# Where layer one's last sums are split, and when layer two's first pair takes its second products

## The chip, the cores and the metric

The kernel runs on one core of one Trainium2 chip. The metric is the device time of one execution in microseconds; less is better. The median of three runs of the kernel before is 566.02 us (565.81 to 566.04).

## What is computed

A retention (a linear attention with a decaying state, 8 heads, 768 steps, batch 2) gives `x`, 1536 tokens of 512 numbers. Two feed-forward layers follow, each 512 to 2048 to 512, in float32:

```python
def _moe_ref(x, w_in, w_out):
    h = x @ w_in
    g = np.maximum(h, 0.0) + np.log1p(np.exp(-np.abs(h)))
    return (g @ w_out).astype(np.float32)
...
def _moe2_ref(x, w_in, w_out, s, b):
    h = x @ w_in
    r = np.maximum(h, 0.0)
    g = s * (r * r) + b
    return (g @ w_out).astype(np.float32)
...
    x = _moe_ref(x=x, **moe_kwargs)
    return _moe2_ref(x=x, **moe2_kwargs)
```

## The kernel before

**Parts.** Every factor of a large product is split into a high part (a rounded copy, `xh`, `wh`, `gh`) and a low part (the rest, `xl`, `wl`, `gl`), and a product is the sum of three: high by high, high by low, low by high. The rounded copy is made on ScalarE and the subtraction mostly on GpSimd (`split`, L110); a weight of 128 x 512 is first put together from two 32-bit words by `split_w` (L277) in four steps: a shift on VectorE (L290); a merge of words on VectorE (L292) with a scaled copy on ScalarE (L295, "the word half") and the load of another raw weight on the SP queue; a second merge on VectorE (L300); and the split.

**Tiles and pairs.** The 1536 tokens are three tiles of 512 (0, 1, 2). The 2048 hidden numbers are taken 128 at a time, and in layer two in pairs of these (p = 0 to 7). For a pair and a tile there are *first products* (the hidden numbers, into one bank of PSUM), the curve (in layer two a relu L559, a square L584, a scaled identity L585, then the split into `gh` and `gl`), and *second products*, which add to four banks of PSUM, the accumulators; there is one set of accumulators. After a pair's two halves, four instructions *take* the accumulators to `xa` of the tile on VectorE (L621 for the first pair, a copy, and L623 later, an addition). A full block of either kind is twelve matmuls of 512 columns.

**The layer change.** Layer one ends with the last steps of tile 2, whose second products run while layer two's first pair has begun. Its sum (accumulators plus what stands in `xa[2]`) is tile 2's input of layer two. The first pair of layer two is done by `plain` (L953, called in L1165), the later pairs by `second` (L981), which saves products by sums of tiles and weights: it starts with half blocks of six matmuls, copies their banks to SBUF on ScalarE (L508, `p1`, `p5`, `u2`) and joins them on VectorE (L552).

`plain` goes through six blocks k = 0 to 5, the halves 0 and 1 of tiles 0, 1 and 2. In this text F0 to F5 are their first products, and Sjh the second products of tile j, half h, of this first pair. A block's first products go to a bank of PSUM from the list `banks` (`h`, `y`, or `third`, written as None), and the relu frees that bank. Per block, in the program's order: the first products (L502), the relu (`begin`), the rest of the curve and the split of `gh` and `gl` (`finish`), the last step of the previous weight split (`end_part`), second products from the list `accs`, three steps of the next weight split (`go(work, 3)`), and sums and parts of tiles (`sums`, `parts`). In block 2 the last second products of layer one (`end`, L1157) come right after F2: two banks, their sums to `xa[2]` on VectorE (`sum_last`, L423), two more banks, their sums, and then `parts_last`: four copies to `xh[2]` on ScalarE (L428) and four subtractions to `xl[2]` on VectorE (L430). F4 and F5 read these.

The order around the change is thus: F0, two blocks of layer one's second products with F1 and F2 between them, `end`, F3, S00, F4, S01 with its four take copies, F5, and then `second` for the next pair (L981): a half block into `h`, copied as `p1`; a half block into `third` (L998), joined with `p1`; S10 (L1003); a half block into `y`, copied as `p5`; one into `h`, copied as `u2`; S11 with its take; two more half blocks; and so on. In the meantime the sum of tiles x4 is made on VectorE in block 3 (L448; its high part `x4h` on ScalarE, L485, and its low parts `x4l` on GpSimd, L488), and two sums of quarters of tile 2 in block 4 (L538).

Each engine works through its own queue in the order of the program (`manual_schedule`); engines wait for each other only where data or a bank, or a buffer, requires it.

Of the kernel before, what the change touches and what calls it, by code (L numbers as in the profile page):

```python
# [7 lines left out]
F32 = mybir.dt.float32  # L8
F32R = mybir.dt.float32r
U32 = mybir.dt.uint32  # L10
AF = mybir.ActivationFunctionType
ALU = mybir.AluOpType
# [10 lines left out]
NTILE = NT // TT  # L23
CPT = TT // C
KC = DM // P
# [23 lines left out]
def tile_retention_mlps(ctx: ExitStack, tc: tile.TileContext, head, w1, w2, sb, out):  # L49
    nc = tc.nc  # L50
# [18 lines left out]
    def bank(pool, tag):  # L69
        return pool.tile([P, 512], F32, tag=tag, name=tag)  # L70
# [19 lines left out]
    xh = [cp.tile([P, KC, TT], F32R, tag=f"xh{j}", name=f"xh{j}") for j in range(NTILE)]  # L90
    xl = [cp.tile([P, KC, TT], F32R, tag=f"xl{j}", name=f"xl{j}") for j in range(NTILE)]
    xa = [cp.tile([P, KC, TT], F32, tag=f"xa{j}", name=f"xa{j}") for j in range(NTILE)]
# [240 lines left out]
    steps = [(0, g, j, f4) for g in range(NG) for j in range(NTILE) for f4 in range(FG)]  # L333
# [7 lines left out]
    h_t, l_t, gg_t, acc_t = {}, {}, {}, {}  # L341
# [76 lines left out]
    def sum_last(banks):  # L418

        la, g, j, _ = steps[NS - 1]  # L420
        for cc in banks:
            t = xa[j][:, cc]
            nc.vector.tensor_tensor(out=t, in0=acc_t[la, g, j][cc], in1=t, op=ALU.add)  # L423

    def parts_last():
        j = NTILE - 1
        for cc in range(KC):
            nc.scalar.activation(xh[j][:, cc], xa[j][:, cc], AF.Copy)  # L428
        for cc in range(KC):
            nc.vector.tensor_tensor(  # L430
                out=xl[j][:, cc], in0=xa[j][:, cc], in1=xh[j][:, cc].bitcast(F32), op=ALU.subtract
            )

    x_t, x3 = {}, {}

# [42 lines left out]
    def parts_x(k, la=1):  # L478
        hi, lo = both(k)
        if k == 3 or k == 4 and not la:  # L480
            src = [x3[c] for c in range(2)]
            for c in range(2):
                nc.scalar.activation(hi[:, c], src[c], AF.Copy)
        else:
            nc.scalar.activation(hi, x_t[k], AF.Copy)  # L485
            src = [x_t[k][:, c] for c in range(2)]
        for c in range(2):
            nc.gpsimd.tensor_tensor(out=lo[:, c], in0=src[c], in1=hi[:, c].bitcast(F32), op=ALU.subtract)  # L488
        x_t[k] = hi, lo
# [9 lines left out]
    def all_of(ps, w, j):  # L499
        ops = [(a, b, k) for k in range(KC) for a, b in ((0, 0), (0, 1))] + [(1, 0, k) for k in range(KC)]  # L500
        for i, (a, b, k) in enumerate(ops):
            nc.tensor.matmul(  # L502
                ps, w[a][:, k * P : (k + 1) * P], (xh, xl)[b][j][:, k], start=i == 0, stop=i == len(ops) - 1
            )
# [41 lines left out]
    def next_t():  # L546
        turn[0] ^= 1
        return tp.tile([P, TT], F32, tag="t2" if turn[0] else "t1", name="c")
# [6 lines left out]
    def begin(la, src, own=False, by_pool=True, tags=None):  # L555

        if la:
            c = src if own else next_t()
            nc.scalar.activation(c, src, AF.Relu)  # L559
            return src, c, None  # L560
        if tags:
            r, u = (late.tile([P, TT], F32, tag=tag, name=tag) for tag in tags)
        else:
            r, u = next_t(), None
        if by_pool:
            nc.scalar.activation(r, src, AF.Relu)
            return src, r, u if tags else src if own else next_t()
        nc.vector.tensor_scalar(
            out=r.bitcast(U32), in0=src.bitcast(U32), scalar1=0x80000000, scalar2=None, op0=ALU.bitwise_or
        )  # L570
        nc.scalar.activation(r, r, AF.Softplus)
        return src, r, None
# [8 lines left out]
    def finish(la, p, half, j, of):  # L581
        src, c, u = of
        if la:
            nc.scalar.activation(c, c, AF.Square)  # L584
            nc.scalar.activation(c, c, AF.Identity, scale=sbt[:, 0:1], bias=sbt[:, 1:2])  # L585
        elif u is not None:
            nc.gpsimd.tensor_tensor(out=c, in0=c, in1=u, op=ALU.add)  # L587
            late_parts.append((la, p, half, j, c))
            return
        else:  # L590
            nc.vector.scalar_tensor_tensor(out=c, in0=src, scalar=0.0, in1=c, op0=ALU.max, op1=ALU.add)
        parts_g(la, p, half, j, c)
# [3 lines left out]
    def parts_g(la, p, half, j, c):  # L596
        gg_t[la, p, half, j] = gh, gl = next_g()
        split(gh, gl, c, nc.scalar, nc.gpsimd)

    def acc_2(la, p, j, half, banks=FIRST + SECOND):  # L600
        wh, wl = w_t[la * NF + 2 * p + half, 1]
        gh, gl = gg_t[la, p, half, j]
        if (la, p, "pair", j) not in acc_t:
            acc_t[la, p, "pair", j] = sums()[0]
        for some in ((0, 1), (2,)):
            for cc in banks:
                cs = slice(cc * P, (cc + 1) * P)
                if la:
                    ops = ((gh[:, cs], wh), (gl[:, cs], wh), (gh[:, cs], wl))
                else:  # L610
                    ops = ((wh[:, cs], gh), (wh[:, cs], gl), (wl[:, cs], gh))
                for i in some:
                    nc.tensor.matmul(  # L613
                        acc_t[la, p, "pair", j][cc], *ops[i], start=half == 0 and i == 0, stop=half == 1 and i == 2
                    )

    def take_2(la, p, j, banks=range(KC)):
        for cc in banks:
            ps, dst = acc_t[la, p, "pair", j][cc], xa[j][:, cc, :]
            if la and p == 0:  # L620
                nc.vector.tensor_copy(dst, ps)  # L621
            else:
                nc.vector.tensor_tensor(out=dst, in0=ps, in1=dst, op=ALU.add)  # L623
            if la and p == PAIRS - 1:
                r0 = j * TT + cc * P
                nc.sync.dma_start(out=out[r0 : r0 + P, :], in_=dst)

    NS = len(steps)
# [54 lines left out]
    def go(work, n):  # L683
        for _ in range(n):
            next(work, None)
# [54 lines left out]
    work, left = [iter(())], [0]  # L740
# [13 lines left out]
    with tc.manual_schedule():  # L754
# [130 lines left out]
        work = iter(())  # L885
# [6 lines left out]
        def part(to):  # L892

            nonlocal late_work, work
            late_work, work = work, split_next(to)
# [8 lines left out]
        def end_part():  # L904
            while late_parts:
                parts_g(*late_parts.pop(0))
            go(late_work, 1)
# [34 lines left out]
        def of_pair(la, p, j, half):  # L942
            def take(banks):
                if half:
                    take_2(la, p, j, banks)

            return lambda banks: acc_2(la, p, j, half, banks), take

        def whole(acc, take):
            acc(FIRST + SECOND)  # L950
            take(FIRST + SECOND)

        def plain(la, p, left, sums, parts):  # L953

            w = la * NF + 2 * p
            base = at[la, p + 1]
            accs = left + [lambda: whole(*of_pair(la, p, 0, 0)), lambda: whole(*of_pair(la, p, 0, 1)), lambda: None]
            banks = [(ps_h, "h"), (ps_y, "y"), None, (ps_h, "h"), None, (ps_y, "y")]
            for k, (j, half) in enumerate((j, half) for j in range(NTILE) for half in range(2)):
                part(base + k + 2 if la or k > 1 else 0)  # L960
                to = bank(*banks[k]) if banks[k] else bank_2[1]
                all_of(to, w_t[w + half, 0], j)
                if la and k == 2:
                    end_part()
                    accs[k]()
                of = begin(la, to, by_pool=False)
                if not la:
                    end_part()
                    go(work, 2)
                finish(la, p, half, j, of)  # L970
                if la:
                    end_part()
                if not la or k != 2:
                    accs[k]()
                go(work, 3 if la else 1)
                for x in sums[k]:
                    next(x, None)
                for x in parts[k]:
                    parts_x(x, la)
# [147 lines left out]
        for s in range(SB, GS):  # L1127
            accs = [of_step(s - LAG)]
# [7 lines left out]
        left = [lambda s=s: whole(*of_step(s)) for s in range(GS - LAG, GS)]  # L1136
# [5 lines left out]
        for s in range(S1, NS):  # L1142
            k = s - S1
            if k < 4:
                accs = [of_pair(0, P1 - 1, 1 + k // 2, k % 2)]
            else:
                accs = [of_step(s - LAG)] if k > 4 else [of_step(S1), of_step(S1 + 1)]
# [15 lines left out]
        left = [lambda s=s: acc_mm(s, FIRST + SECOND) for s in range(NS - LAG, NS - 1)] + [end]  # L1163
# [4 lines left out]
        p = PAIRS - 1  # L1168
# [6 lines left out]
        cc, r0 = KC - 1, NT - P  # L1175
# [90 lines left out]
```

## Time and profile before

| | |
|---|---|
| median of three runs | 566.02 us |
| the profiled execution, its own time | 565.88 us |
| its span in the profile | 564.0 us |
| TensorE busy | 557.2 us, 99% of the span |
| VectorE, ScalarE, GpSimd busy | 68%, 62%, 62% |
| mean granted clock of TensorE | 0.999 |
| chain that ended last | TensorE 92%, GpSimd 4%, ScalarE 2%, VectorE 1% |

The span is the time from the first to the last instruction that the profiler saw; the execution's own time is 1.9 us longer. Times in the rows below count from the start of the span. A timeline row gives the start, the duration, the engine (PE is TensorE, DVE VectorE, ACT ScalarE, POOL GpSimd), the line, the operation, what it writes and reads, and in brackets how long the engine stood still before it and what released it. Neighbouring instructions of one kind are one row ("x4"). Matmuls overlap, so a row's duration is longer than its distance to the next.

### The profile page before, as it was taken

The numbers are of one execution on the slowest core, as the hardware profiler recorded it, in microseconds if no ns is written. First come the engines' busy times: TensorE is split into PE (matmuls) and PEld (weight loads), VectorE is DVE, ScalarE is ACT, GpSimd is POOL, SyncE is SP. The second block draws the span as 40 slices with busy tenths as digits, with TensorE's granted clock in tenths as the row PEclk, the third lists the DMA queues.
The fourth block names the chain that finished last, engine by engine and source line by source line (L and its number), as shares of the span: only waits on it lengthen the run. The fifth ranks groups of instructions, "written<-read, shape, count | busy, mean of one in ns | idle before, by whom it ended". The sixth has DMA issues, their size and how long they took to land.

```text
span 564.0 us, 8397 instructions
## 1 busy us (share of the span) xinstructions
PE 557.2 (99%) x3098; PEld 465.4 (83%) x3098; DVE 383.7 (68%) x581; ACT 349.4 (62%) x641; POOL 348.9 (62%) x293
## 2 busy tenths in 40 slices
PE   8999999999999999999999999999999999999997
PEld 7877888888888888888888777888888888888886
DVE  4887768776757759786859887675665665656334
ACT  3766673544554665543437878858687776868561
POOL 4457467776598797733525999647566555646230
PEclk9999999999999999999999999999999999999999
DMA  8986112101222213322212022222211221110005
GB/s 342 405 355 223 41 38 65 48 29 48 74 76 73 76 37 111 115 76 77 73 38 76 0 74 76 76 74 76 75 63 53 74 74 41 73 38 2 0 11 213
DMA packets 15016, 50.61 MB, mean 90 GB/s; under 512 B 1792, under 2 KB 2048, under 8 KB 14976
## 3 DMA queue, kind: packets, MB, share of 16 engines
q1 hardware_dynamic: 14976, 50.08, 25.1%
q8 instruction: 24, 0.39, 0.3%
q14 instruction: 16, 0.13, 0.1%
HBM read 46.93 MB, written 3.15 MB: 89 GB/s over the span
## 4 chain that ended last, share of the span: by engine, by line
PE 92%; POOL 4%; ACT 2%; DVE 1%; issue 1%; DVEq 0%
PE acc L613 33%; PE acc L403 11%; PE h L494 9%; PE y L494 8%; PE h L352 8%; PE third L494 5%; PE y L352 4%; PE y L502 3%; PE third L502 2%; PE y L191 2%; PE s L172 2%; PE h L502 1%; PE h L191 1%; POOL gl L115 1%; PE acc L775 1%
## 5 line engine op out<-in xcount | busy, mean ns | idle before, releaser
L115 POOL TENSOR_TENSOR wl<-wm,wh 128x512 fp32r<-128x512 f32 x64 | 84.6, 1322 | 101.0 <-ACT wh L112 101.0
L115 POOL TENSOR_TENSOR gl<-c,gh 128x512 fp32r<-128x512 f32 x69 | 91.0, 1324 | 70.3 <-ACT gh L112 48.5
L623 DVE TENSOR_TENSOR xa<-acc,xa 128x512 f32<-128x512 f32 x131 | 82.3, 683 | 71.4 <-PE acc L613 71.2
L613 PE MATMUL acc<-wh,gl 128*128 128x512 f32 x190 | 74.3, 391 | 0.0
L613 PE MATMUL acc<-wh,gh 128*128 128x512 f32 x190 | 74.1, 390 | 0.0
L613 PE MATMUL acc<-wl,gh 128*128 128x512 f32 x190 | 53.9, 390 | 0.0
L112 ACT ACTIVATE gh<-c 128x512 fp32r<-128x512 f32 x69 | 43.6, 632 | 10.9 <-POOL c L587 6.9
L295 ACT ACTIVATE wm<-raw 128x512 f32<-128x512 f32 x64 | 42.4, 663 | 8.7 <-POOL wl L115 8.6
L300 DVE SCALAR_TENSOR_TENSOR wm<-wm,cu,word 128x512 uint32<-128x512 uint32 x54 | 39.9, 739 | 4.1 <-ACT wm L295 3.4
L292 DVE SCALAR_TENSOR_TENSOR word<-raw,cu,word 128x512 uint32<-128x512 uint32 x54 | 40.8, 756 | 1.9
L613 PEld LDWEIGHTS acc<-wl,gh 128*128 128x128 f32 x190 | 35.7, 188 | 7.6
L112 ACT ACTIVATE wh<-wm 128x512 fp32r<-128x512 f32 x64 | 39.7, 620 | 3.2 <-DVE wm L300 3.0
L613 PEld LDWEIGHTS acc<-wh,gl 128*128 128x128 f32 x190 | 35.8, 188 | 6.6
L613 PEld LDWEIGHTS acc<-wh,gh 128*128 128x128 f32 x190 | 35.8, 188 | 6.4
L585 ACT ACTIVATE c<-c,sbt 128x512 f32<-128x512 f32 x48 | 39.2, 816 | 1.6
L365 ACT ACTIVATE t<-t 128x512 f32<-128x512 f32 x24 | 15.1, 629 | 38.9 <-DVE t L359 38.9
L403 PE MATMUL acc<-gh,wh 128*128 128x512 f32 x96 | 37.9, 395 | 0.0
L403 PE MATMUL acc<-gl,wh 128*128 128x512 f32 x96 | 37.4, 390 | 0.0
L613 PE MATMUL acc<-gh,wh 128*128 128x512 f32 x96 | 37.3, 389 | 0.0
L613 PE MATMUL acc<-gl,wh 128*128 128x512 f32 x96 | 37.3, 389 | 0.0
L290 DVE TENSOR_SCALAR word<-raw 128x512 uint32<-128x512 uint32 x54 | 37.0, 686 | 0.4
L559 ACT ACTIVATE c<-c 128x512 f32<-128x512 f32 x21 | 13.1, 633 | 33.6 <-DVE c L552 33.6
(265 smaller groups left out, 1461.4 us busy)
## 6 DMA issues: line engine op xcount, KB each, us to landing
raw<-w SPq DMA_DIRECT2D x64, 512.0 KB, 3.5
qk<-head SPq DMA_DIRECT2D x12, 512.0 KB, 8.3
kv<-head SPq DMA_DIRECT2D x12, 512.0 KB, 8.4
out<-xa SPq DMA_DIRECT2D x11, 256.0 KB, 2.1
cst<-head SPq DMA_DIRECT2D x1, 518.0 KB, 4.4
cst<-head SPq DMA_DIRECT2D x1, 256.0 KB, 5.4
out<-xa SPq DMA_DIRECT2D x2, 128.0 KB, 1.8
sbt<-sb SPq DMA_DIRECT2D x1, 1.0 KB, 10.3
```

The source lines that it names most:

```text
L112: nc.scalar.activation(hi, src, AF.Copy)
L115: lo_eng.tensor_tensor(out=lo, in0=src, in1=hi.bitcast(F32), op=ALU.subtract)
L290: nc.vector.tensor_scalar(out=x, in0=lw, scalar1=29, scalar2=None, op0=ALU.logical_shift_right)
L292: nc.vector.scalar_tensor_tensor(out=x, in0=hw, scalar=cu[:, 0:1], in1=x, op0=ALU.bitwise_and, op1=ALU.bitwise_or)
L295: nc.scalar.activation(m, hw.bitcast(F32), AF.Copy, scale=REBIAS)
L300: nc.vector.scalar_tensor_tensor(out=m.bitcast(U32), in0=m.bitcast(U32), scalar=cu[:, 1:2], in1=x, op0=ALU.logical_shift_left, op1=ALU.bit ...
L352: nc.tensor.matmul(ps, w[:, cc * P : (cc + 1) * P], r[j][:, cc, :], start=i == 0, stop=i == len(ops) - 1)
L403: nc.tensor.matmul(acc_t[la, g, j][cc], *ops[i], start=f4 == 0 and i == 0, stop=ends(s) and i == 2)
L494: nc.tensor.matmul(ps, w[a][:, k * P : (k + 1) * P], x[b][:, k], start=start and i == 0, stop=i == len(ops) - 1, skip_group_check=True,)
L585: nc.scalar.activation(c, c, AF.Identity, scale=sbt[:, 0:1], bias=sbt[:, 1:2])
L613: nc.tensor.matmul(acc_t[la, p, "pair", j][cc], *ops[i], start=half == 0 and i == 0, stop=half == 1 and i == 2)
L623: nc.vector.tensor_tensor(out=dst, in0=ps, in1=dst, op=ALU.add)
```

## The change

Five things, all for layer two's first pair. `sum_last` leaves the sums in the accumulators' banks instead of `xa[2]`. `parts_last` makes the high and low parts from the banks. A new function `whole_last` copies the sums from the banks to `xa[2]` on ScalarE, after block 2's relu. The list of second products is moved one block later: none in block 3, S00 in block 4, S01 and its take in block 5; and to go with it the banks of F4 and F5 are exchanged (F4 to `y`, F5 to `third`). The three split steps of a block come ahead of its second products instead of behind them.

```diff
         la, g, j, _ = steps[NS - 1]
         for cc in banks:
-            t = xa[j][:, cc]
-            nc.vector.tensor_tensor(out=t, in0=acc_t[la, g, j][cc], in1=t, op=ALU.add)
+            t = acc_t[la, g, j][cc]
+            nc.vector.tensor_tensor(out=t, in0=t, in1=xa[j][:, cc], op=ALU.add)
 
     def parts_last():
-        j = NTILE - 1
+        la, g, j, _ = steps[NS - 1]
+        ps = acc_t[la, g, j]
         for cc in range(KC):
-            nc.scalar.activation(xh[j][:, cc], xa[j][:, cc], AF.Copy)
+            nc.scalar.activation(xh[j][:, cc], ps[cc], AF.Copy)
         for cc in range(KC):
-            nc.vector.tensor_tensor(
-                out=xl[j][:, cc], in0=xa[j][:, cc], in1=xh[j][:, cc].bitcast(F32), op=ALU.subtract
-            )
+            nc.vector.tensor_tensor(out=xl[j][:, cc], in0=ps[cc], in1=xh[j][:, cc].bitcast(F32), op=ALU.subtract)
+
+    def whole_last():
+        la, g, j, _ = steps[NS - 1]
+        for cc in range(KC):
+            nc.scalar.activation(xa[j][:, cc], acc_t[la, g, j][cc], AF.Copy)
...
-            accs = left + [lambda: whole(*of_pair(la, p, 0, 0)), lambda: whole(*of_pair(la, p, 0, 1)), lambda: None]
+            own_accs = [lambda: whole(*of_pair(la, p, 0, 0)), lambda: whole(*of_pair(la, p, 0, 1))]
+            accs = left + ([lambda: None] + own_accs if la else own_accs + [lambda: None])
             banks = [(ps_h, "h"), (ps_y, "y"), None, (ps_h, "h"), None, (ps_y, "y")]
+            if la:
+                banks[4:] = banks[:3:-1]
             for k, (j, half) in enumerate((j, half) for j in range(NTILE) for half in range(2)):
...
                 of = begin(la, to, by_pool=False)
+                if la and k == 2:
+                    whole_last()
                 if not la:
                     end_part()
                     go(work, 2)
                 finish(la, p, half, j, of)
                 if la:
                     end_part()
+                    go(work, 3)
                 if not la or k != 2:
                     accs[k]()
-                go(work, 3 if la else 1)
+                if not la:
+                    go(work, 1)
                 for x in sums[k]:
                     next(x, None)
                 for x in parts[k]:
                     parts_x(x, la)
```

## Rows read from the trace of the kernel before

**Rows 1.** The page, part 1: busy us (share of the span) and instructions.

```profile
PE 557.2 (99%) x3098; PEld 465.4 (83%) x3098; DVE 383.7 (68%) x581; ACT 349.4 (62%) x641; POOL 348.9 (62%) x293
```

**Rows 2.** Waits of TensorE, whole span: us in total, times, longest.

```profile
PE h L494 <- ACT p L508: 1.1, 1, 1.1
```

**Rows 3.** Timeline of TensorE: start us, us, engine, line, operation [idle before <-releaser].

```profile
316.58 0.39 PE L502 MATMUL h<-xh,wh 128*128 128x512 f32 x1
...
319.30 0.39 PE L613 MATMUL acc<-wh,gh 128*128 128x512 f32 x1
...
324.18 0.50 PE L502 MATMUL third<-xl,wh 128*128 128x512 f32 x1 [0.41 <-DVE xl L430]
...
336.33 0.39 PE L494 MATMUL y<-x1h,sh 128*128 128x512 f32 x1
...
338.96 0.50 PE L494 MATMUL h<-x2h,sh 128*128 128x512 f32 x1 [1.11 <-ACT p L508]
...
343.91 0.50 PE L494 MATMUL y<-xh,sh 128*128 128x512 f32 x1 [0.57 <-ACT p L508]
...
346.76 0.39 PE L613 MATMUL acc<-wh,gh 128*128 128x512 f32 x1
```

**Rows 4.** Timeline of ScalarE, 318 to 344 us.

```profile
318.48 0.58 ACT L559 ACTIVATE c<-third 128x512 f32<-128x512 f32 x1
...
324.84 0.66 ACT L295 ACTIVATE wm<-raw 128x512 f32<-128x512 f32 x1
327.64 1.06 ACT L485 ACTIVATE x4h<-xa 128x1024 fp32r<-128x1024 f32 x1 [2.14 <-DVE xa L448]
...
332.36 0.58 ACT L559 ACTIVATE c<-y 128x512 f32<-128x512 f32 x1
...
337.23 0.67 ACT L295 ACTIVATE wm<-raw 128x512 f32<-128x512 f32 x1 [1.60 <-POOL wl L115]
...
343.28 0.57 ACT L508 ACTIVATE p<-y 128x512 f32<-128x512 f32 x1
343.76 0.58 ACT L508 ACTIVATE u<-h 128x512 f32<-128x512 f32 x1
```

**Rows 5.** Timeline of VectorE, 317 to 340 us.

```profile
317.82 6.30 DVE L430 TENSOR_TENSOR xl<-xa,xh 128x512 fp32r<-128x512 f32 x4
...
326.31 1.30 DVE L448 TENSOR_TENSOR xa<-xa,xa 128x1024 f32<-128x1024 f32 x1
327.91 2.48 DVE L621 COPY xa<-acc 128x512 f32<-128x512 f32 x4 [0.30 <-PE acc L613]
...
332.54 0.75 DVE L300 SCALAR_TENSOR_TENSOR wm<-wm,cu,word 128x512 uint32<-128x512 uint32 x1 [0.75 <-ACT wm L295]
333.21 2.84 DVE L538 TENSOR_TENSOR xa<-xa 128x512 f32<-128x512 f32 x2
...
336.69 0.76 DVE L292 SCALAR_TENSOR_TENSOR word<-raw,cu,word 128x512 uint32<-128x512 uint32 x1
...
338.94 0.69 DVE L552 TENSOR_TENSOR c<-third,p 128x512 f32<-128x512 f32 x1 [0.25 <-ACT p L508]
```

**Rows 6.** Timeline of GpSimd at 331 us.

```profile
331.23 2.56 POOL L488 TENSOR_TENSOR x4l<-xa,x4h 128x512 fp32r<-128x512 f32 x2
```

**Rows 7.** Groups of VectorE by form: line, operation, count | busy us, mean ns.

```profile
L552 DVE TENSOR_TENSOR third<-third,p 128x512 f32<-128x512 f32 x3 | 2.1, 700 | 2.9 <-ACT p L508 2.1 <-PE third L494 0.8
```

**Rows 8.** Stretches at the end: us, busy by engine, granted clock (PEclk), DMA, GB/s.

```profile
561.00:562.00 1.00, 0.00 (x0) 0.00 (x0) 0.42 (x1) 0.00 (x0) 0.00 (x0) 1.00 1.00 368
...
563.00:564.00 1.00, 0.00 (x0) 0.00 (x0) 0.00 (x0) 0.00 (x0) 0.00 (x0) 0.64 0.00 0
```

**Rows 9.** Timeline of TensorE, the first 10 us.

```profile
1.45 2.93 PE L775 MATMUL acc<-xa 128*128 128x128 f32 x12 [1.45 <-DVE xa L757]
4.32 1.22 PE L172 MATMUL s<-qk 64*128 64x128 f32 x8
...
8.94 0.72 PE L172 MATMUL s<-qk 64*128 64x128 f32 x8
```

## The prediction

> **What bounds the kernel now.** The page's first part comes first: TensorE is busy for nearly the whole span [rows 1], so the end moves only by what TensorE loses or regains. Its table of waits then shows how little there is to regain, and that it lies at the layer change [rows 2]. TensorE's timeline puts numbers on it [rows 3]. A block of twelve matmuls takes 2.72 us (316.58 to 319.30). From 316.58 to 346.76 there are ten blocks' worth of matmuls (F3, S00, F4, S01, F5, the two half blocks of the next pair, S10, two halves, S11, two halves), 27.20 us, in 30.18: 2.98 us are lost. F4 loses its part at 324.18, where it waits for the last low part `xl` of tile 2; the rest goes at 338.96 and 343.91, where the next pair waits for copies (`p`) late on ScalarE. From S10's end at 336.33 to 346.76 stand 10.43 us for 8.16 of work: 2.27 lost there. The three waits in brackets are 2.09 of it; the rest, about 0.3 a time, is restarting.
>
> Then ScalarE's and VectorE's timelines, to see who is late [rows 4, 5]. Between its relu of F2 (318.48) and that of F5 (332.36) ScalarE stands still only once, for 2.14 us, until VectorE has summed x4. F5 was over at 330.89 (336.33 less two blocks): its relu was already 1.5 us behind TensorE. The reader is to see that ScalarE's queue, not TensorE's, sets the pace here, and that VectorE's merge at 332.54 waits for it.
>
> **What goes.** The four `xl` subtractions took 6.30 us out of SBUF [rows 5]. With one source in the accumulators I price them like the four copies out of the same banks, 2.48 us [rows 5]; the sums that now stay in the banks cost 0.70 each, as the join that writes its own bank [rows 7]. The parts are then ready by 317.9 + 2.5 = 320.4. F4 now follows F3 directly, at 319.30, and needs its first `xl` one matmul (0.23 us) later, its last at 320.9: in time by some 0.5 us. The 0.70 us at F4 goes.
>
> **What is added.** Four copies of the sums to `xa` on ScalarE, between F2's relu and its square. Two such copies out of banks start 0.48 apart and last 0.57 to 0.58 [rows 4]: between 1.9 and 2.4 us, and I take 2.0, the timeline's spacing. They end at 319.06 + 2.0 = 321.1; S00, which overwrites the banks, is now at 322.02, so they are not on TensorE's path there. But everything behind them on ScalarE moves by 2.0. The one idle stretch doesn't absorb it: word half at 324.84, merge on VectorE, sum of x4, `x4h` at 327.64 is one chain [rows 4, 5], so all of it comes 2.0 later, and F5's relu runs from 334.36 to 334.94. VectorE being free 3.7 us sooner buys nothing, since its next merge waits for that word half.
>
> **What is moved, and past what.** TensorE now runs F3, F4, S00, F5, S01 and the next pair's first half block without a wait: 316.58 + 5 x 2.72 + 1.36 = 331.54. Then comes the half block into `third`. Before, F4 was the last user of that bank; now F5 is, and its relu ends at 334.94. **First wait: 3.4 us.** The half block ends near 336.3.
>
> S10 comes next and wants the accumulators. They are emptied by S01's four take copies, which before stood right behind S01 on VectorE (327.91, 0.30 us after a wait for TensorE) and ahead of that block's weight splits [rows 5]. Now they stand in F5's block, and behind its three split steps, the last of which is a merge that waits for ScalarE. I walk VectorE's queue. The merge of F4's block moves by 2.0, from 332.54 to 334.54. Behind it are the two tile sums of L538, at 335.2; before they took 2.84 us beside a busy GpSimd, while the sum of x4, twice the width, took 1.30 [rows 5], so two take between 1.3 and 2.84. GpSimd needs about 1.3 us for one low part (`x4l`, two in 2.56 [rows 6]); after `x4h` it has two `x4l`, `gl` and `wl`, to about 335.9, then nothing until F5's `gh` near 337.1. So VectorE has it beside itself for only part, and I take 1.9. From the end of these sums (336.05) to that of the second split step (336.69 + 0.76) were 1.40: here 338.5. F5's word half, freed of its 1.60 us wait for GpSimd [rows 4], would be at 335.6 + 2.0 and ends at 338.3, so the merge runs 338.5 to 339.2, and the takes from 339.2 to 341.7. **Second wait:** S10 starts at 339.85 on the first bank, gets the last at 341.7, and still has six matmuls (1.36) to do: it ends at 343.1 instead of 336.33, 6.8 us later. It had waited 3.5 us.
>
> What is late next? The join behind the takes comes at 341.7 instead of 338.94, 2.8 later, so `p5`, kept at 343.28 to 343.85 before [rows 4], is there by 346.7; TensorE wants it at 343.1 + 5.44 = 348.5. So the 2.27 us lost there before vanish: 6.8 - 2.27 = **+4.5 us**. The take of tile 1 and the steady pairs keep their order. The weight loads on SP keep theirs too, with nothing moved past them; they follow the splits.
>
> Bounds: the copies -0.1 to +0.4, the tile sums -0.2 (then the word half decides) to +0.9: 4.2 to 5.8.
>
> **The clock.** Two waits of 3.4 and 3.5 us with one half block between them are new to TensorE. At the end of the span the matmuls are over by 561; in the slice 563 to 564 the granted clock is 0.64, a mixture of 2.4 and 1.2 GHz [rows 8]. Two to three idle microseconds were enough there, so I expect it to fall here as well. The start shows the lower level and the climb: the same eight matmuls take 1.22 us at 4.32 and 0.72 at 8.94, the first matmul being at 1.45 [rows 9]; the full rate thus came between 4.1 us (5.54) and 7.5 us (8.94) after it. S10 would start low. Each microsecond at 1.2 GHz loses half a microsecond; of this 0.5 is free, because S10 would have spent 3.25 us on its 2.72 of work anyway. I take 4 us low, the short end of those rows, since S10 follows on other matmuls and not on a start from nothing: 2.0 - 0.5 = **+1.5**; bounds 0 (it doesn't fall) and 7.5 / 2 - 0.5 = 3.2. The Trainium skill ("TensorE: Matmul & The Clock Gate", section "HAM oscillation — how this bites in real kernels") says that idle stretches of the array bring the slow clock back and are paid again each time. By that rule the sum would be the one with this term, 571.9; without it 570.4. The trace agrees as far as it goes, with 0.64 in that slice.
>
> **The sum.** 4.5 + 1.5 = 6.0 on the profiled execution, whose own time is 565.88 (0.14 under the median of the runs): 571.9 us.
>
> **Rivals.**
> - The clock stays up: 565.88 + 4.5 = 570.4, from 570.1 to 571.7. For it: one half block breaks the idle time. Against it: rows 8. Chance 0.18.
> - Only the first wait comes true, because the takes meet free accumulators in time; that needs the last bank free by 337.7, so the merge ahead of them at 334.5 instead of 338.5. S10 would end at 339.0, 2.7 later, less 2.27: 566.3, no change that can be told. Nothing in VectorE's order supports it. 0.05.
> - **Faster**: all 2.98 us come back and nothing takes their place, 562.9. The place is F5's relu: it must end by 331.54. It ended at 332.94 before, without the copies, so ScalarE would have to gain 1.4 and lose nothing for 2.0 more, and the takes must be early too. For it speaks only that GpSimd's and VectorE's slow operations on SBUF shorten; ScalarE does not wait for these in that stretch, but for the one chain. 0.05.
> - The change does not do what it says for F4: if `xl` out of the banks still took 6.30 in all, it would be ready at 324.1 against 320.9, and F4 would lose 3.2. The wait at `third` would shrink by the same: still 571.9. It is in the forecast's chance.
> - Worse: the low clock lasts, or a further wait follows the two: 574.5 to 576. 0.07.
>
> **The numbers.** The forecast (both waits and the slow clock) has 0.65, with its own range of 570.4 (a short dip) to 574.9 (every bound at its upper end); the steadier clock 0.18. From 570.1 to 574.4 both are held but for those upper ends together: about 8 in 10, and that is the range. This kernel's measurement tells some 0.2% (1.1 us) from no change: slower 0.65 + 0.18 + 0.07 = 0.90, same 0.05, faster 0.05.
>
> **What would show it.** Right: no wait for `xl` at F4; four ScalarE copies behind F2's relu; TensorE waiting some 3.4 us at a `third` matmul for the relu (L559) and again about 3.5 us at S10's accumulators for the take copies; no waits for `p` behind; the granted clock under 1.00 around 340. Wrong, if the first wait is under 1 us, if the takes come straight behind S01, if the clock never leaves 1.00, or if TensorE gets a new wait in a later pair.

## The result, and the profile after

The changed kernel takes 572.8 us (median of four runs, 572.67 to 573.25) against 565.91 for the kernel before on the same chips (565.8 to 566.04): a ratio of 1.0123, 95% interval 1.0105 to 1.0141. It is slower, by 6.9 us; 571.9 was forecast, with 570.1 to 574.4 as the range. The profiled execution took 572.68, with a span of 570.8, against 565.88 and 564.0. One execution of a version below, the takes ahead of the splits, took 1591.2 us at a mean granted clock of 0.344 and is left out of that version's figures. In the changed kernel most lines of `plain` and its helpers stand four lines further down (L613 is now L617, L621 L625, L494 L498, L508 L512, L552 L556, L559 L563).

TensorE's table of waits (us in total, times, longest), its two largest; before, this stretch had two for `p` and one for `xl` [rows 2, 3]:

```profile
PE third L498 <- ACT c L563: 3.3, 1, 3.3
PE acc L617 <- DVE xa L625: 2.8, 1, 2.8
```

Both waits for `p` and the one for `xl` are gone; two larger ones have come. TensorE's timeline:

```profile
316.74 0.39 PE L506 MATMUL h<-xh,wh 128*128 128x512 f32 x1
...
319.46 0.39 PE L506 MATMUL y<-xh,wh 128*128 128x512 f32 x1
...
330.34 0.39 PE L498 MATMUL h<-xh,wh 128*128 128x512 f32 x1
...
335.18 0.79 PE L498 MATMUL third<-xh,wh 128*128 128x512 f32 x1 [3.32 <-ACT c L563]
...
340.93 0.50 PE L617 MATMUL acc<-wh,gh 128*128 128x512 f32 x1 [2.83 <-DVE xa L625]
...
345.36 0.39 PE L498 MATMUL y<-x1h,sh 128*128 128x512 f32 x1
...
353.52 0.39 PE L617 MATMUL acc<-wh,gh 128*128 128x512 f32 x1
```

F4 follows F3 at 319.46 with no wait for `xl` (F3 starts 0.16 us later than in [rows 3], a shift from ahead of the changed part). The first half block of the next pair is at 330.34. The half block into `third` waits 3.32 us for F5's relu, S10 2.83 us for the take copies, and S10 ends at 345.36. From there to 353.52 stand 8.16 us, the work alone. Before, S10 ended at 336.33, so it is 9.03 us later. Less the 0.16, and less the 2.27 that the kernel before lost behind S10 and this one doesn't, 6.6 us are left of the 6.8 between the two profiled executions; the 0.16 is the rest. So the difference lies in this stretch.

ScalarE's timeline, to be held against [rows 4]:

```profile
317.04 2.07 ACT L429 ACTIVATE xh<-acc 128x512 fp32r<-128x512 f32 x4 [2.66 <-DVE acc L423]
318.97 0.64 ACT L563 ACTIVATE c<-third 128x512 f32<-128x512 f32 x1
319.49 2.08 ACT L436 ACTIVATE xa<-acc 128x512 f32<-128x512 f32 x4
...
327.20 0.65 ACT L295 ACTIVATE wm<-raw 128x512 f32<-128x512 f32 x1
329.86 1.06 ACT L489 ACTIVATE x4h<-xa 128x1024 fp32r<-128x1024 f32 x1 [2.00 <-DVE xa L452]
...
334.55 0.57 ACT L563 ACTIVATE c<-third 128x512 f32<-128x512 f32 x1
```

The four copies to `xa` are the third row: 2.08 us, between the relu of F2 and its square. From there everything is late: the word half at 327.20 instead of 324.84, `x4h` at 329.86 instead of 327.64, F5's relu at 334.55 instead of 332.36. The bracket of the first row is worth a second look: ahead of the high parts ScalarE stood still for 2.66 us, with F2 already finished. VectorE's timeline, beside [rows 5]:

```profile
318.16 2.48 DVE L431 TENSOR_TENSOR xl<-acc,xh 128x512 fp32r<-128x512 f32 x4
...
327.94 0.75 DVE L300 SCALAR_TENSOR_TENSOR wm<-wm,cu,word 128x512 uint32<-128x512 uint32 x1 [5.90 <-ACT wm L295]
...
334.73 0.75 DVE L300 SCALAR_TENSOR_TENSOR wm<-wm,cu,word 128x512 uint32<-128x512 uint32 x1 [3.52 <-ACT wm L295]
335.40 2.03 DVE L542 TENSOR_TENSOR xa<-xa 128x512 f32<-128x512 f32 x2
...
338.93 0.75 DVE L300 SCALAR_TENSOR_TENSOR wm<-wm,cu,word 128x512 uint32<-128x512 uint32 x1
339.60 2.48 DVE L625 COPY xa<-acc 128x512 f32<-128x512 f32 x4
```

The four `xl` take 2.48 us instead of 6.30. After two more split steps VectorE then stands still for 5.90 us, until the word half: the time won has become a wait. The merge of F4's block waits again for ScalarE (3.52 us). Then the queue runs as a chain, tile sums, splits, merge, and only behind it the take copies, at 339.60; before they stood at 327.91.

The granted clock in the stretches of the two waits (columns: stretch, its us, then busy us and count of PE, PEld, DVE, ACT and POOL, then PEclk, DMA share, GB/s):

```profile
331.00:334.00 3.00, 0.86 (x4) 0.38 (x2) 0.22 (x1) 2.90 (x6) 2.86 (x3) 1.00 0.00 0
334.00:335.00 1.00, 0.00 (x0) 0.00 (x0) 0.27 (x1) 1.00 (x3) 1.00 (x2) 0.81 0.00 0
335.00:338.00 3.00, 2.82 (x6) 1.82 (x6) 2.97 (x4) 2.90 (x6) 1.78 (x2) 0.50 0.56 175
...
339.00:341.00 2.00, 0.07 (x1) 0.07 (x1) 2.00 (x4) 0.38 (x1) 2.00 (x2) 1.00 0.50 178
341.00:342.00 1.00, 1.00 (x4) 0.79 (x5) 1.00 (x3) 0.00 (x0) 0.12 (x1) 0.72 0.43 168
342.00:344.00 2.00, 2.00 (x6) 1.62 (x5) 1.97 (x5) 1.29 (x3) 0.06 (x1) 0.50 0.03 8
...
345.00:348.00 3.00, 3.00 (x15) 2.49 (x14) 0.39 (x1) 1.99 (x4) 2.25 (x3) 1.00 0.00 0
```

1.00 is 2.4 GHz, 0.50 is 1.2. The clock fell in the slice from 334 to 335, in the first wait, and the half block into `third` ran at the lower level. It was back at 1.00 by 339, while TensorE stood in the second wait. It fell again between 341 and 342, with S10 just begun, until it was back at 345. Most of S10 ran at the lower level.

### The profile page after: what moved, and what is told of

It is laid out like the page before. It is cut to its first block, busy times and chain, and to the rows that moved or that the text cites. A ratio compares the mean times of both kernels' runs of the same rounds, so it can differ in the third digit from the quotient of the medians.

```text
span 570.8 us, 8401 instructions
## 1 busy us (share of the span) xinstructions
PE 559.9 (98%) x3098; PEld 467.4 (82%) x3098; DVE 378.0 (66%) x581; ACT 350.9 (61%) x645; POOL 344.8 (60%) x293
## 4 chain that ended last, share of the span: by engine, by line
PE 93%; ACT 4%; DVE 1%; DMA 1%; issue 0%; DVEq 0%
PE acc L617 34%; PE acc L403 11%; PE h L498 9%; PE y L498 8%; PE h L352 8%; PE third L498 5%; PE y L352 4%; PE third L506 3%; PE y L506 3%; PE y L191 2%; PE s L172 2%; PE h L506 1%; PE h L191 1%; PE acc L172 1%; DMA qk<-head 1%; ACT c L589 1%
## 5 line engine op out<-in xcount | busy, mean ns | idle before, releaser
L617 PE MATMUL acc<-wh,gh 128*128 128x512 f32 x190 | 74.9, 394 | 2.8 <-DVE xa L625 2.8
L617 PE MATMUL acc<-wh,gl 128*128 128x512 f32 x190 | 75.1, 395 | 0.0
L617 PE MATMUL acc<-wl,gh 128*128 128x512 f32 x190 | 54.3, 392 | 0.0
L617 PEld LDWEIGHTS acc<-wh,gh 128*128 128x128 f32 x190 | 36.1, 190 | 10.0 <-DVE xa L625 3.6
L617 PEld LDWEIGHTS acc<-wl,gh 128*128 128x128 f32 x190 | 36.1, 190 | 7.8
L617 PEld LDWEIGHTS acc<-wh,gl 128*128 128x128 f32 x190 | 36.2, 191 | 6.7
L617 PE MATMUL acc<-gh,wh 128*128 128x512 f32 x96 | 37.3, 389 | 0.0
L617 PE MATMUL acc<-gl,wh 128*128 128x512 f32 x96 | 37.3, 389 | 0.0
L563 ACT ACTIVATE c<-c 128x512 f32<-128x512 f32 x21 | 13.1, 633 | 39.0 <-DVE c L556 39.0
```

The lines of the kernel that those rows point to most:

```text
L617: nc.tensor.matmul(acc_t[la, p, "pair", j][cc], *ops[i], start=half == 0 and i == 0, stop=half == 1 and i == 2)
```

## The experiments

Edits are against the changed kernel unless a line says otherwise. A trace can be shifted as a whole against another; the start of the half block into `h`, 330.34 in the changed kernel, shows by how much. It is 330.16 for the takes ahead of the splits and 330.05 for the filled waits.

### One part of the change undone

**Takes ahead of the splits again.**

```diff
                 if la:
                     end_part()
-                    go(work, 3)
                 if not la or k != 2:
                     accs[k]()
-                if not la:
-                    go(work, 1)
+                go(work, 3 if la else 1)
```

> Changed kernel, but with each block's second products and take copies ahead of its three split steps again, as before. Theory (queues: the takes of S01 stand behind a merge that waits for ScalarE): the takes start when the two tile sums end, near 337.4 instead of 339.6, so S10 starts 2.2 us earlier, near 338.7; the first wait, at third, stays 3.3 us. The time falls by 1.3 to 2.4 us, to 570.4 to 571.5 (the clock's second dip decides within that). Rival (the takes are late whatever stands ahead of them, since VectorE waits for ScalarE in any order): 572.8, S10 still at 340.9.

Measured: 571.38 us (median of three runs, 570.63 to 572.57); ratio to before 1.0093 (1.0069 to 1.0117). The profiled execution took 571.38. First VectorE's, then TensorE's timeline, then the granted clock:

```profile
337.16 2.48 DVE L625 COPY xa<-acc 128x512 f32<-128x512 f32 x4
```

```profile
334.99 0.80 PE L498 MATMUL third<-xh,wh 128*128 128x512 f32 x1 [3.31 <-ACT c L563]
...
338.49 0.80 PE L617 MATMUL acc<-wh,gh 128*128 128x512 f32 x1 [0.57 <-DVE xa L625]
...
343.78 0.63 PE L498 MATMUL y<-x1h,sh 128*128 128x512 f32 x1
```

```profile
334.00:335.00 1.00, 0.01 (x1) 0.01 (x1) 0.45 (x1) 0.97 (x3) 1.00 (x2) 0.68 0.00 0
335.00:344.00 9.00, 8.43 (x19) 6.21 (x20) 8.79 (x14) 5.62 (x10) 4.98 (x5) 0.50 0.37 118
344.00:345.00 1.00, 1.00 (x4) 0.79 (x4) 0.96 (x2) 0.97 (x2) 1.00 (x1) 0.70 0.01 4
```

The takes start at 337.16 and S10 at 338.49, as the queue said; the rival falls. The gain, 1.4 us, is smaller than the 2.4 us (2.3 less the shift) by which S10 starts earlier: in this trace the granted clock stayed at 0.50 from 335 to 344, so S10 took 5.3 us (338.49 to 343.78), about twice its 2.72. The runs spread over some 2 us (570.63 to 572.57), where the filled version below, whose clock stays up, spreads over 0.2.

**Banks as before** (F4 to `third`, F5 to `y`).

```diff
-            if la:
-                banks[4:] = banks[:3:-1]
```

> Changed kernel, but F4 goes to third and F5 to y, as before. Theory (the first wait is hidden behind the second, because S10 waits for the takes in any case): the wait of 3.3 us at third goes nearly whole, the wait at the accumulators grows by about as much, S10 still starts near 340.9, time 572.2 to 573.2. Rival (the two waits add up): the 3.3 us come back, 569.5. F4 may wait 0.2 us for F2's relu in third.

Measured: 572.62 us, ratio 1.0114 (1.0098 to 1.0131). The waits of TensorE:

```profile
PE acc L617 <- DVE xa L625: 7.3, 1, 7.3
```

The wait at `third` is gone, and the one at the accumulators has grown from 2.83 to 7.34 us. The time stays. The first wait of the changed kernel costs nothing by itself: S10 would not start sooner without it. Two waits in a row on one engine don't add up where the second ends at a time that the first doesn't move.

**The copies to `xa` on VectorE.**

```diff
-            nc.scalar.activation(xa[j][:, cc], acc_t[la, g, j][cc], AF.Copy)
+            nc.vector.tensor_copy(xa[j][:, cc], acc_t[la, g, j][cc])
```

> Changed kernel, but the four copies of the sums to xa are made by VectorE behind the four xl subtractions, not by ScalarE. Theory (the four ScalarE copies push everything behind them by 2.0 us, and VectorE is idle there): relu of F5 ends 2.0 us earlier, first wait 1.3 us, takes and S10 2.0 us earlier, time 570.0 to 571.3, or 1.5 us less if the clock then stays up. Rival (the order of the blocks alone costs the time, the copies nothing): 572.8.

Measured: 571.23 us, ratio 1.0095 (1.0072 to 1.0118), at the upper end of what was expected. The profiled execution started 1.9 us late as a whole (its half block into `h` is at 332.25), so times are read less 1.9. Its word half is 1.8 us earlier than in the changed kernel, nearly all of the 2.0; but `x4h` only 1.3, because the sum of x4 now takes longer on VectorE:

```profile
328.72 1.68 DVE L452 TENSOR_TENSOR xa<-xa,xa 128x1024 f32<-128x1024 f32 x1
```

1.68 us instead of 1.22: moved forward, it meets GpSimd at work. TensorE waits 1.99 us at `third` and 4.10 at the accumulators, and S10 starts 1.3 us earlier. The copies do push the chain, but of the 1.8 us won by moving them a quarter is lost again at the next engine.

**The waits filled with matmuls.** Thirty multiplications whose results nothing reads, into the bank `y`.

```diff
+            def idle(n):
+                for _ in range(n if la and p == 1 else 0):
+                    nc.tensor.matmul(other, ah[:, :P], xh[0][:, 0], start=True, stop=True, skip_group_check=True)
+
             six(one, a11, b11, True)
             p1 = kept(one, "p1")
+            idle(13)
             six(third, a12, b21, True)
+            idle(17)
```

> Changed kernel with thirty extra matmuls into the bank y, which is free there: 13 ahead of the half block into third, 17 behind it, at 0.227 us each just short of the two waits; their results are overwritten. They add work and wait for nothing new. Theory (1.5 to 2 us of the loss are S10 at 1.2 GHz): the granted clock stays at 1.00, S10 starts at 340.9 as before and ends near 343.5 instead of 345.4, time 570.7 to 571.3. Rival (the slow clock costs nothing, or S10 is slow for another reason such as the take copies on its banks): 572.8 or more.

Measured: 570.81 us (570.79 to 571.02), ratio 1.0082 (1.0063 to 1.01). TensorE's timeline, and the granted clock of the stretch in which S10 ends:

```profile
331.41 3.11 PE L1009 MATMUL y<-xh,wh 128*128 128x512 f32 x13
334.89 0.50 PE L498 MATMUL third<-xh,wh 128*128 128x512 f32 x1 [0.36 <-ACT c L563]
...
336.38 4.04 PE L1009 MATMUL y<-xh,wh 128*128 128x512 f32 x17
340.67 0.50 PE L617 MATMUL acc<-wh,gh 128*128 128x512 f32 x1 [0.25 <-DVE xa L625]
...
343.52 0.39 PE L498 MATMUL y<-x1h,sh 128*128 128x512 f32 x1
```

```profile
342.00:344.00 2.00, 2.00 (x11) 1.65 (x10) 1.97 (x4) 1.56 (x3) 0.33 (x1) 1.00 0.00 0
```

S10 takes 2.85 us (340.67 to 343.52) instead of 4.43, at 1.00. Thirty matmuls more, 6.8 us of work, and the kernel is 2.0 us faster by the medians; the runs spread over 0.2 us. That is what the slow clock cost, or a little less: S10 is 1.58 us shorter, and 0.29 of the difference between the two profiled executions (572.68 and 570.81) is a shift from ahead of this stretch. The waits themselves, without the clock, are the other 4.9 to 5.0 us.

### One part of the change alone

**Parts from the accumulators alone** (order of blocks, banks and splits as before).

```diff
-            accs = left + ([lambda: None] + own_accs if la else own_accs + [lambda: None])
+            accs = left + own_accs + [lambda: None]
```

(and the two edits above that put the takes and the banks back)

> The kernel before with only the parts taken from the accumulators (sums left in the banks, four ScalarE copies to xa); order of blocks, banks and splits as before. Theory (the queues add up): S00 directly behind F3 now finds banks still being copied and waits 1.2 us; the 0.7 us at F4 goes; ScalarE is 2.0 us later, so the copies p1 and p5 come later and the two old waits for them stay, near 1 us each. Time 566.3 to 567.5. Rival (this half of the change is a gain by itself, all of the loss is in the new order): 564.5 to 565.3.

Measured: 566.45 us against 565.72, ratio 1.0012 (1.0003 to 1.0021). The waits of TensorE:

```profile
PE acc L617 <- ACT xa L436: 1.0, 1, 1.0
PE h L498 <- ACT p L512: 0.9, 1, 0.9
PE y L498 <- ACT p L512: 0.7, 1, 0.7
```

S00, directly behind F3, finds the banks still being copied; the two waits for `p` stay. The rival, a gain from this half alone, falls.

**The new order alone** (against the kernel before: the edits of `plain` without `whole_last`; parts from `xa`).

```diff
-            accs = left + [lambda: whole(*of_pair(la, p, 0, 0)), lambda: whole(*of_pair(la, p, 0, 1)), lambda: None]
+            own_accs = [lambda: whole(*of_pair(la, p, 0, 0)), lambda: whole(*of_pair(la, p, 0, 1))]
+            accs = left + ([lambda: None] + own_accs if la else own_accs + [lambda: None])
...
+            if la:
+                banks[4:] = banks[:3:-1]
...
                 if la:
                     end_part()
+                    go(work, 3)
```

> The kernel before with only the new order (second products one block later, banks of F4 and F5 exchanged, split steps ahead of second products); parts from xa as before, no copies on ScalarE. Theory: F4 waits some 3 us for xl, relu of F5 is early enough, so no wait at third; the takes stand behind the merge near 338.6 and S10 starts near 340, with 4 us idle and one dip of the clock; time 569.5 to 571.8. Rival (the ScalarE copies are what costs, the new order nothing): 566.0.

Measured: 571.5 us, ratio 1.0101 (1.0082 to 1.012). Waits:

```profile
PE acc L613 <- DVE xa L621: 3.4, 1, 3.4
PE y L502 <- DVE xl L430: 2.5, 3, 1.0
```

No wait at `third`, since ScalarE has no copies to make; F4 waits 2.5 us for `xl` instead, and S10 for the takes as in the changed kernel. So the parts alone cost 0.7 us, the order alone 5.8, and both 6.9: the order is what costs. How much of that is the place of the takes alone no run separates. Ahead of the splits, but still in block 5, they give back 1.4 us; in block 4 they were run only with the old banks and the old place of the splits as well (566.45 above, and the next version).

### Towards a faster version

**F2's curve ahead, S01 in block 4.** ScalarE's 2.66 idle us are filled with the curve of F2, and both second products with their takes go where the takes stood before.

```diff
-            accs = left + ([lambda: None] + own_accs if la else own_accs + [lambda: None])
+            both_accs = lambda: (own_accs[0](), own_accs[1]())
+            accs = left + ([lambda: None, both_accs, lambda: None] if la else own_accs + [lambda: None])
...
-                if la and k == 2:
-                    end_part()
-                    accs[k]()
                 of = begin(la, to, by_pool=False)
-                if la and k == 2:
-                    whole_last()
                 if not la:
                     end_part()
                     go(work, 2)
                 finish(la, p, half, j, of)
                 if la:
                     end_part()
-                    go(work, 3)
-                if not la or k != 2:
-                    accs[k]()
-                if not la:
-                    go(work, 1)
+                accs[k]()
+                if la and k == 2:
+                    whole_last()
+                go(work, 3 if la else 1)
```

(banks as before)

> Parts from the accumulators and copies on ScalarE as in the changed kernel, but: F2's curve goes ahead of the last sums on ScalarE (in the 2.7 us in which it stood idle), S00 and S01 with its takes both stand in block 4 (F3, F4, S00, S01, F5), ahead of that block's split steps, and F4 and F5 have their banks as before. Theory: no wait at F4, third or S10; p1 and p5 still 0.3 to 1 us late each; clock 1.00; time 564.0 to 565.2, faster than before. Rival (ScalarE is too late in any order once it makes four more copies): 566 or more, with a wait at third or at S10.

Measured: 565.11 us against 565.72, ratio 0.999 (0.998 to 0.9999). ScalarE's timeline:

```profile
314.12 0.58 ACT L563 ACTIVATE c<-third 128x512 f32<-128x512 f32 x1
...
316.87 2.07 ACT L429 ACTIVATE xh<-acc 128x512 fp32r<-128x512 f32 x4
319.31 2.07 ACT L436 ACTIVATE xa<-acc 128x512 f32<-128x512 f32 x4 [0.38 <-DVE xl L431]
```

The relu of F2 is at 314.12, in the gap; its whole curve is done when the high parts begin at 316.87 (317.04 in the changed kernel, whose trace is 0.18 us later here). No wait at F4, `third` or S10; those for `p` remain, 0.84 and 0.72 us.

**And the copies on VectorE.** (The edit of `whole_last` above.)

> As e7_take_in_block4, and the four copies to xa are made by VectorE behind xl. Theory: ScalarE gains 2 us more, p1 and p5 are in time, nearly all 2.98 us lost at the layer change come back: 562.9 to 563.8. Rival (GpSimd, which makes the low parts, or VectorE is next to be late, and p1 with it): the same as e7_take_in_block4 or slower.

Measured: 564.54 us against 565.72, ratio 0.9986 (0.9977 to 0.9996): better than both kernels, but 0.7 us above the range that was expected. The waits for `xl` and for `p1` are gone; one for `p5` is left. TensorE's timeline, then VectorE's:

```profile
342.42 0.50 PE L498 MATMUL y<-xh,sh 128*128 128x512 f32 x1 [1.41 <-ACT p L512]
```

```profile
332.46 2.83 DVE L542 TENSOR_TENSOR xa<-xa 128x512 f32<-128x512 f32 x2
...
337.45 0.68 DVE L556 TENSOR_TENSOR c<-third,p 128x512 f32<-128x512 f32 x1
338.05 3.19 DVE L542 TENSOR_TENSOR xa<-xa 128x512 f32<-128x512 f32 x2
```

`p5` stands behind c11's curve on ScalarE, and that curve waits 1.71 us for c11's join on VectorE (337.45). The join stands behind two L542 sums, which take 2.83 us, and the split steps after them; `p1`, which it also needs, is there at 336.46. So the rival, VectorE next to be late, holds in part. Two L542 sums took 1.41 us when GpSimd stood still (in the changed kernel, at 342.59); the pair behind the join takes 3.19, with GpSimd at work for some 2.2 us of it. The Trainium skill ("SBUF — State Buffer", section "SBUF: two separate sides") says that VectorE with two inputs in SBUF and a GpSimd instruction that reads SBUF share one pair of ports, held by one of them for a whole instruction. The pairs of durations here agree with that.

**`p5` and `u2` ahead of c11's curve**, on the version above and on the kernel before.

```diff
             whole(*of_pair(la, p - 1, 1, 0))
-            finish(la, p, 0, 0, c11)
+            if not la or p > 1:
+                finish(la, p, 0, 0, c11)
             go_last()
             if la and p == 1:
                 sum_z((2, 4))
-                parts_z(3)
...
             u2 = kept(one, "u2")
+            if la and p == 1:
+                finish(la, p, 0, 0, c11)
+                parts_z(3)
```

> As e8_and_whole_on_vector; in the next pair ScalarE also copies p5 and u2 before it squares, scales and splits c11 (and before the parts of z3), where these stood ahead of p5. Theory (the one wait left, 1.41 us and a restart at the matmuls into y, is p5 queued behind c11's curve on ScalarE): that wait goes, 1.4 to 1.6 us less than e8_and_whole_on_vector, 562.8 to 563.2, 0.5% under the kernel before. Rival (c11's low part, later now, or VectorE's sums of tiles are next to be late): 564 or more, with a new wait in S11 or behind it.

Measured: 564.74 us against 565.84, ratio 0.9982 (0.9973 to 0.9991): not to be told from the version without it (0.9986). TensorE's timeline:

```profile
343.97 0.50 PE L617 MATMUL acc<-wh,gh 128*128 128x512 f32 x1 [0.16 <-DVE xa L625]
...
355.63 0.39 PE L498 MATMUL y<-xh,sh 128*128 128x256 f32 x1 [0.69 <-ACT p L512]
```

The wait of 1.41 us is gone, and two others stand later, 0.16 at the take and 0.69 in the last tile. The rival holds: what was won came back.

> The kernel before with only that order of p5, u2 and c11's curve. Theory (the losses at the layer change are separate terms: 0.70 at F4, 1.40 at p1, 0.87 at p5): 0.87 us less, 564.7 to 565.1, with the waits at F4 and p1 as they were. Rival (they hang together: p5 comes late because p1 does): no change, 565.7 to 566.0.

Measured: 565.06 us against 565.84, ratio 0.9987 (0.9978 to 0.9996). The waits at F4 (0.41) and at p1 (1.08) are as before, that at p5 is gone, and 0.8 us with it: here the term was separate.

**The tile sums for z2 and z4 later** (on the version with `p5` ahead: `sum_z((2, 4))` behind the joins of c12 and c22, their parts behind c22's curve).

```diff
             c22 = begin(la, joined(one, p5), own=True)
+            if la and p == 1:
+                sum_z((2, 4))
...
             finish(la, p, 1, 1, c22)
+            if la and p == 1:
+                parts_z(2)
+                parts_z(4)
```

> As e9_p5_ahead; the two tile sums for z2 and z4 (L542, 3.19 us on VectorE ahead of tile 1's take there) and their parts go behind the joins of c12 and c22. Theory (what e9_p5_ahead won came back because VectorE reached the take and the joins late, behind these sums): the take starts as S11 ends, the joins come 1.6 us earlier, the waits of 0.16 and 0.69 us go, 563.2 to 563.8. Rival (ScalarE is late in the last tile whatever VectorE does, now with two more splits ahead of its copies): 564.4 or more, with a wait at the half blocks into y of the last tile.

Measured: 567.99 us against 565.94, ratio 1.0039 (1.0023 to 1.0054): far from the theory, and without the wait that the rival names. The sums themselves take 1.41 us there, and the joins are early. But the last tile's take writes `xa[2]`, which GpSimd must first have read for the low parts of z. VectorE's timeline, then TensorE's:

```profile
355.35 2.52 DVE L625 COPY xa<-acc 128x512 f32<-128x512 f32 x4 [6.51 <-POOL xl L115]
```

```profile
356.79 0.72 PE L617 MATMUL acc<-wh,gh 128*128 128x512 f32 x1 [3.37 <-DVE xa L625]
```

The take waits 6.51 us for that low part, and TensorE 3.37 us for the take; the granted clock behind this wait is 0.50 from 357 to 360. A bound that nobody had on the list: a buffer that is free only when the parts made from it are done.

## Why the prediction was right

Its steps, less the 0.16 us of a later start:

- **F4**: `xl` was priced at 2.5 us and took 2.48; no wait. Right.
- **ScalarE's four copies**: 2.0 forecast, 2.08 measured; F5's relu at 334.4 against 334.36. Right, and by the mechanism named: the idle stretch that is part of the same chain absorbs next to nothing (2.14 us before, 2.00 now).
- **First wait**: 3.4 us forecast, 3.32 measured. What the forecast left unsaid is that it costs nothing, as the run with the old banks shows.
- **Takes behind the splits**: 339.2 forecast, 339.4 measured; the tile sums took 2.03 us where 1.9 was taken between 1.3 and 2.84.
- **S10's start**: 339.85 forecast, 340.8 measured. This step failed in part: S10 did not start on the first bank. The first two accumulators are one tile in the program (`acc01` in `sums`, L72), and S10 began when two copies were done. Most of it was given back, since S10 then no longer waits for the last bank: with the clock up it ended at 343.52, where 343.1 was forecast.
- **No waits behind**: right; both waits for `p` are gone.
- **The clock**: +1.5 forecast; 2.0 by the filled kernel's median, 1.6 by S10's length (4.43 against 2.85). That it falls was argued from [rows 8] and came true. The size came out near, but its course was not the one forecast, so the size is in part luck. The 4 us were taken from durations in [rows 9]; the granted clock reads 1.00 in every microsecond of that stretch, so that the first matmuls ran at the lower level is not shown. And how long a low spell lasts varied: over 9 us with the takes ahead of the splits. The forecast had one spell of 4 us from before S10 on. There were two: the first fell on the half block into `third` and cost nothing, since S10 had to wait anyway; the second began when S10 had begun. It also named "under 1.00 around 340" as a sign, and at 340 the clock stood at 1.00. The Trainium skill ("TensorE: Matmul & The Clock Gate", section "HAM oscillation — how this bites in real kernels") says that a fall is paid for again each time. Both dips here did slow the matmuls behind them, to 0.43 us apart; only the second moved the end.

In sum 4.5 + 1.5 = 6.0 was forecast, and 6.9 measured: 4.9 + 2.0 by the filled kernel's median. By the traces, with S10's length from the filled kernel, it is 5.0 + 1.6 and the 0.16 of the later start. So the takes and S10's start account for 0.4 to 0.5 of the difference, and the clock for 0.1 to 0.5. The rivals fell by the changed kernel's own trace: the clock left 1.00, the takes stand at 339.60, F4 doesn't wait, and no new wait follows the two.

What stays open: why the clock's dips fall where they do from one execution to the next; no run here tells. The runs of the versions with dips spread over up to 2.9 us (the order alone, 569.85 to 572.71), those of the filled one over 0.2; that the dips make this spread is likely, not shown.

## What to carry to other kernels

Before work is made cheaper on one engine, look at what its next instruction waits for: here VectorE won 3.8 us and spent 5.9 waiting for ScalarE, which had been given four more copies. When a step that frees a buffer is moved, walk the queue that it now stands in to its last wait; the takes were late not for their own 2.5 us but for the merges and sums ahead of them. And fill an idle gap with what the late engine needs anyway: with the parts alone the kernel took 566.45 us, and with F2's curve in such a gap and S00 one block later besides, 565.11; how much of these 1.3 us each of the two gave, no run tells.

## What the runs showed of the hardware that was not expected

- Thirty extra matmuls in two waits made the kernel 1.6 to 2.0 us faster, since the granted clock stayed at 1.00. Without them the second wait cost its own length and, behind it, matmuls at 1.2 GHz: the 512-column ones started 0.43 us apart (341.53, 341.96, 342.39) instead of 0.23.
- With a wait of 3.31 us and then one of only 0.57 the clock stayed at 0.50 for over 9 us (takes ahead of the splits; TensorE was busy for 8.43 of the 9.00 from 335 to 344), longer than either dip of the changed kernel with its 2.83 us wait. The shorter wait bought less than its length for that reason.
- The same two sums of tiles on VectorE took 1.41 us with GpSimd idle (the changed kernel, at 342.59) and up to 3.21 with GpSimd at work beside them (F2's curve ahead, at 338.73). The sum of x4, moved forward by 1.8 us into GpSimd's work, took 1.68 instead of 1.22.
